# Expert stages of a fused fp32 kernel: A22 in the slots of w_in, sums in the slots of moe1, last output tiles one by one, another matmul step for the scheduler

## The chip, the cores and the metric

The kernel runs on one core of a Trainium2 chip. The metric is the device time of one execution in microseconds; one execution was also profiled, and all rows below are from that one. TensorE is called PE here, VectorE DVE, ScalarE ACT, GpSimd POOL, and the queue that issues the transfers SP.

## What is computed

Attention with a tanh cap on the scores, then two experts, one after the other, all in fp32 (cut from the reference; sizes in the comments):

```python
# q, k, v: 4 batches x 12 heads x 448 x 64
scores = cap * np.tanh(scale * np.matmul(q, k.transpose(0, 1, 3, 2)) / cap)
attn = softmax(scores) @ v                   # heads side by side: x, 1792 x 768
# expert 1, d_ff 2048
h = x @ w_in
y = (h * np.cos(h)) @ w_out
# expert 2, d_ff 1024
a = y @ w1
b = y @ w2
out = ((a * b) @ w3) @ w_out2
```

## The kernel before

A tile has 128 partitions; a batch's 448 tokens lie along the free axis, and the 768 columns of the model are six blocks of 128 rows. Each fp32 matmul is made of three fp32r ones: every operand is held as a rounded high half and the low rest (names ending in h and l), and `mm3` (L377) multiplies high by high, high by low and low by high. So every operand costs a conversion: a cast for the high half (on ACT, DVE or POOL) and a subtraction for the low one (on DVE or POOL), made by `halves`, `copy` (L353), `tt` (L363) and `lo` (L371).

The stages run in this order: attention (`columns`), with `make_w34` (L880 and on), which folds w3 and w_out2 of expert 2 into w34, beside it; `moe1`, expert 1; `moe2`, expert 2.

`moe1` goes through 32 units (a pair of blocks of d_ff, one batch). A unit makes h on PE, copies it into hs, and gets g = h cos h in a chain of DVE and ACT work (`chain`, L954 to L981): w from hs, kk and w less kk (the range reduction), a sine on ACT, times h, then the two halves of g. `y_part` adds g times w_out to y, two units later, and after a batch's last unit each of its six y blocks is stored to DRAM (y_d).

`moe2` takes y from y_d. It treats two batches at once (p = 0: batches 0 and 1, p = 1: batches 2 and 3) with a seven-product scheme: `lefts` makes the left operands A11, A12, S1 to S4 and A22 out of y and its sums, `rights` the right ones out of w1 and w2 for a block fc of d_ff, and `ab_step(p, fc)` multiplies them: seven products of nine matmuls, whose sums leave PSUM as tmp (copies) and c (the products a times b of the two batches, c11 and c21). `o_unit(b, fc)` converts c into the halves ab, loads w34[fc] through stq, and adds w34[fc] times ab to the six output blocks m of batch b, three matmuls each; after fc = 7 a block is copied into ob and stored (outT). For one batch of the pair the units run between the products of the next step, for the other behind the pair's last step.

No stage issues an instruction by itself. Everything goes into a `Plan` with a due time, a cost for each engine that can do it, and its reads and writes. `schedule` plays the plan through with these costs and so fixes the order on each engine; PE's cost is counted in units of `MM`, its time for one matmul of 448 columns. A ring is a number of equal slots; an operation that needs a slot of a full ring waits, in the plan and on the chip. Rings lie in pools, and a pool opens only after every user of the pools that it takes the place of is done (`swap`): mp (weights, hs, w and g of moe1), yp (y) and wi (w_in) close together, and q2 opens in their place. q2 holds what only `moe2` has: stq, rawq, A22's halves, w34, ab, c, tmp and ob. The pool lp (rawl, stl and the other left operands) opens earlier. The lines that decide it are three:

```python
swap("wp", opens=("yp", "mp", "cv"))
swap("cv", "attn", opens=("lp",))
swap("mp", "yp", "wi", opens=("q2",))
```

Of the kernel before, what the change touches and what calls it, by code (L numbers as in the profile page):

```python
# [10 lines left out]
F32 = mybir.dt.float32  # L11
# [317 lines left out]
def program(  # L329
# [52 lines left out]
    MM = S / 2400 + 0.017  # L382
# [10 lines left out]
    for name, kw in dict(const={}, xring={}, dram=dict(space=DRAM), psum=dict(space=PSUM), attn={}, lp={},  # L393
                         wi=dict(side="right"), wp=dict(side="right"), yp=right, mp=right, cv=right,
                         q2=right).items():
        pool(name, **kw)
# [474 lines left out]
    def make_w34():  # L871
# [12 lines left out]
        for k, (fc, p) in enumerate(runs):  # L884
# [9 lines left out]
            for n in range(2):  # L894
                half = slice(n * (DM // 2), (n + 1) * (DM // 2))
                acc = hy_r.ref()
                for q, jc in enumerate(jcs):
# [5 lines left out]
                    plan.op(due + n * 4 + q, [("PE", 3 * (DM / 4800 + 0.017), f)], r=[*w3, *wo[jc]], w=[acc])  # L903
# [15 lines left out]

    def moe1(raw_r, x_r):  # L920
# [3 lines left out]
        hs_r, w_r = (ring("mp", t, [P, 2, S], F32, 2) for t in ("hs", "w"))  # L924
        kk_r = ring("mp", "kk", [P, S], F32, 1)
        g_r = ring("mp", "g", [P, 2, 2, S], F32R, 2, 16)
        y_r = ring("yp", "y", [P, KD, S], F32, 2)
# [105 lines left out]
        for u in (n - 2, n - 1):  # L1033
            for m in range(KD):
                y_part(u, m, unit_due(n) + ((u - n + 2) * KD + m) * pu / 12)
# [10 lines left out]
    KH, HALF = KD // 2, DM // 2  # L1046
# [4 lines left out]
    def moe2():  # L1051
        raws = [ring("lp", "rawl", [P, 2 * DM], U32, 1), ring("q2", "rawq", [P, 2 * DM], U32, 1)]
        sts = [ring("lp", "stl", [P, DM], F32, 4), ring("q2", "stq", [P, DM], F32, 2)]
        left_r = {x: hl("q2" if x == "A22" else "lp", f"y{x}", [P, KH, S], 1, 16 * (x == "A22")) for x in LEFT}
        w34_r, ab_r = hl("q2", "w34", [P, DM], 3), ring("q2", "ab", [P, 2, S], F32R, 3, 16)
        c_r, tmp_r, ob_r = (ring("q2", t, [P, S], F32, n) for t, n in (("c", 11), ("tmp", 6), ("ob", 5)))
        V0, AB, OU = unit_due(4 * NP) + G["pu"], 63 * MM, 18 * MM
        left, right, cs = {}, {}, {}

# [4 lines left out]
        def lefts(p, due, step, raw_r, st_r, late=False):  # L1064

            for x in LEFT:
                if (x == "A22") == late:
                    left[p, x] = [r.new() for r in left_r[x]]
            for k in range(KH):
                t = due + k * step  # L1070

                def to(x, src, at):
                    halves(at, [z.at(k, lambda t, k=k: t[:, k, :]) for z in left[p, x]], src, S)
# [5 lines left out]
                if late:  # L1079
                    a22 = st_r.ref()[:, :S]  # L1080
# [22 lines left out]
        def rights(p, fc, due):  # L1103

            x = [sts[0].ref(), sts[0].ref()]
            for a in range(2):
                z = w12_d.at((fc, a), lambda d, a=a: d[fc, a])
                if p == 0:
                    convert(due + 2 * a, raws[a if fc else 0], x[a], w12[fc, a], DM)
# [24 lines left out]
        def product(p, fc, i, bank, first, due):  # L1134
# [4 lines left out]
            def f():  # L1139
                xt = [z.tile() for z in x]  # L1140
                wt = [seg(z, j, 1) for z in w]
                for k in range(KH):
                    c = slice(k * P, (k + 1) * P)
                    mm3(bank()[:, :S], wt[0][:, c], wt[1][:, c], xt[0][:, k, :], xt[1][:, k, :],
                        first and k == 0, k == KH - 1, on=not first)

            plan.op(due, [("PE", 9 * MM, f)], r=[*(z.at(k) for z in x for k in range(KH)), *(z.at(2 * (j // 2)) for z in w)],
                    w=[bank])

        def ab_step(p, fc, due, between):  # L1150
# [3 lines left out]
            def out(bank, when):  # L1154
                x = tmp_r.ref()
                copy(when, x, bank[:, :S], S, "AD", psum=True)
                return x

            p1 = hy_r.ref()
            product(p, fc, 0, p1, True, at[0])  # L1160
            s1 = out(p1, at[1])
            p2 = hy_r.ref()
# [123 lines left out]
```

## Time and profile before

| | |
|---|---|
| median of 3 runs | 1114.83 us (1112.88 to 1116.92) |
| profiled execution, its own time | 1116.46 us |
| its span | 1114.7 us |
| mean granted TensorE clock | 0.993 |
| PE busy | 1078.9 us, 97%, 5040 matmuls |
| DVE busy | 885.6 us, 79% |
| ACT busy | 498.4 us, 45% |
| POOL busy | 156.1 us, 14% |

The span is the time from the first to the last event of the profiled execution, and its own time is 1.8 us more. Shares of busy time are means over stages with different limits. PE is the engine with almost no idle, so the places to look at are those where a row of PE shows idle time ahead of it, with the operation that ended it, and those where the granted clock is below 1.00 (0.50 is 1.2 of 2.4 GHz).

### The profile page before, as it was taken

The page shows a single profiled execution, that of the slowest core. Times are in us where ns is not written, and L with a number is a line of the kernel's source. Part 1 is how long each engine was busy: PE and PEld are TensorE (multiplying, and loading weights), DVE is VectorE, ACT ScalarE, POOL GpSimd, SP SyncE. Part 2 cuts the span into 40 slices and gives each one's busy share as a digit, 9 for nine tenths or more (in the row PEclk, how much of TensorE's full clock was granted, in tenths as well). Part 3 has the DMA queues.
Part 4 walks back from the last instruction along what each step waited for, and adds up shares of the span by engine and source line. Part 5 has one row for each costly group of instructions (what it writes and reads, how often), then busy time and mean ns, then how long its engine had stood idle before and what let it go on. Part 6 is the DMA issues. An engine that isn't in the chain of part 4 may idle for free. (4 is left out here: it accounts for less than half of the span.)

```text
span 1114.7 us, 13997 instructions
## 1 busy us (share of the span) xinstructions
PE 1078.9 (97%) x5040; PEld 937.4 (84%) x5040; DVE 885.6 (79%) x1353; ACT 498.4 (45%) x656; POOL 156.1 (14%) x145
## 2 busy tenths in 40 slices
PE   5999999999999999999999999999899999999997
PEld 3777777777888888889999999999789998999996
DVE  6988767798998989868789977777699879767642
ACT  4887767677665656641253211111244334221121
POOL 2322111112331111101002000000122200100000
PEclk9999999999999999999999999999999999999998
DMA  9885766877755655426633411204456435421132
GB/s 238 231 221 158 207 186 170 228 192 238 236 165 158 185 151 174 160 75 213 231 124 110 138 48 57 57 15 154 154 184 198 157 116 188 159 85 58 58 107 81
DMA packets 95554, 169.04 MB, mean 152 GB/s; under 512 B 37362, under 2 KB 68850, under 8 KB 95474
## 3 DMA queue, kind: packets, MB, share of 16 engines
q1 hardware_dynamic: 95474, 168.05, 50.1%
q8 instruction: 41, 0.67, 0.3%
q14 instruction: 39, 0.32, 0.1%
HBM read 129.30 MB, written 38.62 MB: 151 GB/s over the span
## 5 line engine op out<-in xcount | busy, mean ns | idle before, releaser
L617 PE MATMUL bank<-p,v 112*128 112x448 f32 x384 | 160.9, 542 | 0.3 <-POOL raw L826 0.3
L606 ACT ACTIVATE double<-double,ts 112x896 f32<-112x896 f32 x96 | 94.1, 981 | 76.2 <-PE double L597 76.0
L378 PE MATMUL bank<-xh,wih 128*128 128x448 f32 x270 | 107.8, 399 | 2.7 <-DVE xh L355 2.2
L617 PEld LDWEIGHTS bank<-p,v 112*128 112x128 f32 x384 | 72.7, 191 | 41.3 <-issue 38.7
L378 PE MATMUL bank<-g,woh 128*128 128x448 f32 x260 | 100.7, 387 | 0.0
L379 PE MATMUL bank<-xl,wih 128*128 128x448 f32 x270 | 98.1, 363 | 0.2 <-DVE xl L364 0.2
L380 PE MATMUL bank<-xh,wil 128*128 128x448 f32 x270 | 98.0, 363 | 0.0
L606 ACT ACTIVATE p<-double,pac 112x896 f32<-112x896 f32 x96 | 96.8, 1011 | 2.4 <-PE bank L617 0.4
L380 PE MATMUL bank<-g,wol 128*128 128x448 f32 x260 | 94.2, 362 | 0.0
L379 PE MATMUL bank<-g,woh 128*128 128x448 f32 x260 | 94.1, 362 | 0.0
L596 PE MATMUL double<-qh,ks 128*112 128x448 f32 x192 | 72.8, 379 | 13.6 <-DVE ks L364 9.5
L364 DVE TENSOR_TENSOR y<-bank,y 128x448 f32<-128x448 f32 x111 | 68.5, 617 | 21.8 <-PE bank L380 21.3
L597 PE MATMUL double<-ql,ks 128*112 128x448 f32 x192 | 71.7, 373 | 0.0
L378 PEld LDWEIGHTS bank<-xh,wih 128*128 128x128 f32 x270 | 50.7, 188 | 11.7 <-issue 5.0
L379 PEld LDWEIGHTS bank<-xl,wih 128*128 128x128 f32 x270 | 50.8, 188 | 8.8 <-issue 5.2
L378 PE MATMUL bank<-w2h,w3h 128*128 128x384 f32 x128 | 57.5, 449 | 0.0
L831 POOL TENSOR_SCALAR wx<-rawc 128x768 f32<-128x768 f32 x29 | 33.7, 1164 | 165.9 <-DVE wil L364 81.7
L354 ACT COPY hs<-bank 128x448 f32<-128x448 f32 x39 | 20.8, 533 | 77.0 <-PE bank L380 76.9
L379 PEld LDWEIGHTS bank<-g,woh 128*128 128x128 f32 x260 | 48.8, 188 | 6.7 <-issue 3.5
L378 PEld LDWEIGHTS bank<-g,woh 128*128 128x128 f32 x260 | 48.8, 188 | 6.6 <-issue 2.8
L380 PEld LDWEIGHTS bank<-xh,wil 128*128 128x128 f32 x270 | 50.8, 188 | 3.4
L976 ACT ACTIVATE w<-w 128x896 f32<-128x896 f32 x32 | 30.5, 953 | 50.5 <-DVE w L364 50.4
(286 smaller groups left out, 2831.7 us busy)
## 6 DMA issues: line engine op xcount, KB each, us to landing
rawc<-in_w_out SPq DMA_DIRECT2D x16, 768.0 KB, 5.9
stq<-w_d SPq DMA_DIRECT2D x32, 384.0 KB, 3.3
qr<-in_q SPq DMA_DIRECT2D x48, 224.0 KB, 5.2
kr<-in_k SPq DMA_DIRECT2D x48, 224.0 KB, 4.8
rawc<-in_w_in SPq DMA_DIRECT2D x13, 768.0 KB, 4.9
raw<-in_w3T SPq DMA_DIRECT2D x16, 512.0 KB, 5.9
rawl<-in_w SPq DMA_DIRECT2D x9, 768.0 KB, 4.5
raw<-in_w_out SPq DMA_DIRECT2D x8, 768.0 KB, 7.5
```

The source lines that it names most:

```text
L354: "A": ("ACT", (0.051 if psum else 0.094) + n / 1200, lambda: ACT.copy(dst(), src())),
L364: "D": ("DVE", 0.068 + n / 960, lambda: DVE.tensor_tensor(dst(), a(), b(), op=op))
L378: PE.matmul(out, wh, xh, start=first, stop=False, skip_group_check=on)
L379: PE.matmul(out, wh, xl, start=False, stop=False, skip_group_check=on)
L380: PE.matmul(out, wl, xh, start=False, stop=last, skip_group_check=on)
L596: PE.matmul(o, w, qh(), start=True, stop=False)
L597: PE.matmul(o, w, ql(), start=False, stop=True)
L606: lambda f=f, x=x, o=o: ACT.activation(o(), s(), f, scale=x[:CP]))],
L617: PE.matmul(pv()[:, :S], w()[:, 2 * c + n].rearrange("p a d -> p (a d)"), p()[:, n, :], start=c == 0 and n == 0, stop=c == NT - 1 and n == 1)
L831: lambda: POOL.tensor_scalar(x(), h_().bitcast(F32), 0.0, 1.0, op0=ALU.mult, op1=ALU.mult)),
L976: plan.op(due + 5, [("ACT", 0.094 + 2 * S / 1200, lambda: ACT.activation(w2(), w2(), AF.Sin, scale=TWOPI))], r=[w2], w=[w2], table="sin")
```

## The change

It joins the two expert stages in memory. The pools of w_in, y and a new one, hp, with hs and w, stay open to the end, and q2 takes the place of mp alone. A22's halves then lie in three slots of w_in's ring; the copies out of PSUM (tmp before) and the loads of A22 lie in halves of hs and w (`spares`); c lies in two y tiles at fixed places (`c_at`); ab is one tile of six parts, used in turn, and ob has three slots instead of five. The last unit's six `y_part` are handed to `moe2`, which plans them ahead of its own work. In `ab_step` the output blocks are planned between the products, not behind them. The last three units of the last batch (LAST = 3) are planned tile by tile: for each m the chunks fc = 5, 6 and 7, where all six m of one chunk came before the next. The raw w1 and w2 of fc = 1 both pass through rawl, where w2's passed through rawq. And two costs are set anew: `MM` from 0.2037 to 0.2000 us, and a matmul of w34 from 0.177 to 0.1733 us.

```diff
...
@@ -379,7 +380,7 @@
         PE.matmul(out, wh, xl, start=False, stop=False, skip_group_check=on)
         PE.matmul(out, wl, xh, start=False, stop=last, skip_group_check=on)
 
-    MM = S / 2400 + 0.017
+    MM = (S + 32) / 2400
     MT = CP / 1200 + 0.002
 
 
@@ -391,7 +392,7 @@
 
     right = dict(side="right", reuse_waits="tile")
     for name, kw in dict(const={}, xring={}, dram=dict(space=DRAM), psum=dict(space=PSUM), attn={}, lp={},
-                         wi=dict(side="right"), wp=dict(side="right"), yp=right, mp=right, cv=right,
+                         wi=dict(side="right"), wp=dict(side="right"), yp=right, hp=right, mp=right, cv=right,
                          q2=right).items():
         pool(name, **kw)
 
@@ -900,7 +901,7 @@
                         mm3(acc()[:, :DM // 2], w3[0]()[:, j], w3[1]()[:, j], wo[jc][0]()[:, half],
                             wo[jc][1]()[:, half], q == 0, q == NJ - 1)
 
-                    plan.op(due + n * 4 + q, [("PE", 3 * (DM / 4800 + 0.017), f)], r=[*w3, *wo[jc]], w=[acc])
+                    plan.op(due + n * 4 + q, [("PE", 3 * (DM / 4800 + 0.0133), f)], r=[*w3, *wo[jc]], w=[acc])
                 o = Ref(sums[fc], n, lambda t, half=half: t[:, half])
                 a = acc[:, :DM // 2]
                 if p == 0:
@@ -917,14 +918,15 @@
     def unit_due(u):
         return G["m0"] + min(u, G["ua"]) * G["pa"] + max(u - G["ua"], 0) * G["pu"]
 
+    y_r = ring("yp", "y", [P, KD, S], F32, 2)
+    hs_r, w_r = (ring("hp", t, [P, 2, S], F32, 2) for t in ("hs", "w"))
+
     def moe1(raw_r, x_r):
         cv = ring("cv", "rawc", [P, 2 * DM], U32, 2)
         wx = ring("mp", "wx", [P, DM], F32, 2)
         wo_r = hl("mp", "wo", [P, DM], 4)
-        hs_r, w_r = (ring("mp", t, [P, 2, S], F32, 2) for t in ("hs", "w"))
         kk_r = ring("mp", "kk", [P, S], F32, 1)
         g_r = ring("mp", "g", [P, 2, 2, S], F32R, 2, 16)
-        y_r = ring("yp", "y", [P, KD, S], F32, 2)
         w_t, g_t, yacc = {}, {}, {}
 
         groups = [(n, (b, b + 1)) for b in range(0, B, BH) for n in range(NP)]
@@ -1030,9 +1032,9 @@
                 chain(u, c, hp[:, :S], u0 + (c + 1) * pu / 2)
         n = len(units)
         weights(NG, unit_due(n) - G["wlead"])
-        for u in (n - 2, n - 1):
-            for m in range(KD):
-                y_part(u, m, unit_due(n) + ((u - n + 2) * KD + m) * pu / 12)
+        for m in range(KD):
+            y_part(n - 2, m, unit_due(n) + m * pu / 12)
+        return [lambda due, m=m: y_part(n - 1, m, due) for m in range(KD)]
 
     def mm_h(hp, wi, ks, xh_, xl_):
         def f():
@@ -1043,19 +1045,33 @@
         return f
 
 
-    KH, HALF = KD // 2, DM // 2
+    KH, HALF, LAST = KD // 2, DM // 2, 3
     LEFT = ("A11", "A12", "S2", "S1", "S3", "S4", "A22")
     RIGHT = ("B11", "B21", "T1", "T3", "T2", "T4", "B22")
     PRODUCTS = (("A11", "B11"), ("A12", "B21"), ("S2", "T2"), ("S1", "T1"), ("S3", "T3"), ("S4", "B22"), ("A22", "T4"))
 
-    def moe2():
+    def moe2(tail):
         raws = [ring("lp", "rawl", [P, 2 * DM], U32, 1), ring("q2", "rawq", [P, 2 * DM], U32, 1)]
         sts = [ring("lp", "stl", [P, DM], F32, 4), ring("q2", "stq", [P, DM], F32, 2)]
-        left_r = {x: hl("q2" if x == "A22" else "lp", f"y{x}", [P, KH, S], 1, 16 * (x == "A22")) for x in LEFT}
-        w34_r, ab_r = hl("q2", "w34", [P, DM], 3), ring("q2", "ab", [P, 2, S], F32R, 3, 16)
-        c_r, tmp_r, ob_r = (ring("q2", t, [P, S], F32, n) for t, n in (("c", 11), ("tmp", 6), ("ob", 5)))
+        left_r = {x: hl("lp", f"y{x}", [P, KH, S], 1) for x in LEFT if x != "A22"}
+        w34_r, abt = hl("q2", "w34", [P, DM], 3), ring("q2", "ab", [P, 6, S], F32R, 1, 16).new()
+        ob_r = ring("q2", "ob", [P, S], F32, 3)
+        abs_ = itertools.cycle(range(3))
         V0, AB, OU = unit_due(4 * NP) + G["pu"], 63 * MM, 18 * MM
         left, right, cs = {}, {}, {}
+
+        def spares():
+            for r in itertools.cycle((hs_r, w_r)):
+                it = r.new()
+                for n in range(2):
+                    yield it.at(n, lambda t, n=n: t[:, n, :])
+
+        spares = spares()
+        low, high = y_r.new(), y_r.new()
+
+        def c_at(b, fc):
+            it, n = (low, fc % 4) if b % 2 == 0 else (high, fc) if fc < KD else (low, fc - KD + 4)
+            return it.at(n, lambda t: t[:, n, :])
 
         def halves(due, z, src, n):
             copy(due, z[0], src, n, "ADP")
@@ -1065,19 +1081,23 @@
 
             for x in LEFT:
                 if (x == "A22") == late:
-                    left[p, x] = [r.new() for r in left_r[x]]
+                    if late:
+                        left[p, x] = [[r.ref()[:, :S] for _ in range(KH)] for r in wi_r]
+                    else:
+                        left[p, x] = [[z.at(k, lambda t, k=k: t[:, k, :]) for k in range(KH)]
+                                      for z in [r.new() for r in left_r[x]]]
             for k in range(KH):
                 t = due + k * step
 
                 def to(x, src, at):
-                    halves(at, [z.at(k, lambda t, k=k: t[:, k, :]) for z in left[p, x]], src, S)
+                    halves(at, [z[k] for z in left[p, x]], src, S)
 
                 def load(x, n, m):
                     src = y_d.at((2 * p + n, m), lambda d: d[2 * p + n, m])
                     dma(t - 4, x, src, r=[src], w=[x], kb=230)
 
                 if late:
-                    a22 = st_r.ref()[:, :S]
+                    a22 = next(spares)
                     load(a22, 1, k + KH)
                     to("A22", a22, t)
                     continue
@@ -1106,7 +1126,7 @@
             for a in range(2):
                 z = w12_d.at((fc, a), lambda d, a=a: d[fc, a])
                 if p == 0:
-                    convert(due + 2 * a, raws[a if fc else 0], x[a], w12[fc, a], DM)
+                    convert(due + 2 * a, raws[a if fc > 1 else 0], x[a], w12[fc, a], DM)
                     dma(due - 4, z, x[a], r=[x[a]], w=[z], kb=393, write=True)
                 else:
                     dma(due - 12, x[a], z, r=[z], w=[x[a]], kb=393)
...
         def ab_step(p, fc, due, between):
@@ -1152,40 +1172,48 @@
             at = [due + i * (AB + OU) / 7 for i in range(8)]
 
             def out(bank, when):
-                x = tmp_r.ref()
+                x = next(spares)
                 copy(when, x, bank[:, :S], S, "AD", psum=True)
                 return x
+
+            def then(i):
+                if i < len(between):
+                    between[i](at[i + 1] + 0.1)
 
             p1 = hy_r.ref()
             product(p, fc, 0, p1, True, at[0])
             s1 = out(p1, at[1])
+            then(0)
             p2 = hy_r.ref()
             product(p, fc, 1, p2, True, at[1])
-            c11 = c_r.ref()
+            c11 = c_at(2 * p, fc)
             tt(at[2], c11, p2[:, :S], s1, S, ALU.add, psum=True)
+            then(1)
             product(p, fc, 2, p1, False, at[2])
             u2 = out(p1, at[3])
+            then(2)
             p3 = hy_r.ref()
             product(p, fc, 3, p3, True, at[3])
             s5 = out(p3, at[4])
+            then(3)
             product(p, fc, 4, p1, False, at[4])
             tt(at[5], s5, p1[:, :S], s5, S, ALU.add, psum=True)
+            then(4)
             product(p, fc, 5, p3, False, at[5])
             tt(at[6], u2, p3[:, :S], u2, S, ALU.add, psum=True)
             tt(at[6] + 1, c11, c11, u2, S, ALU.mult, "DP")
+            then(5)
             product(p, fc, 6, p1, False, at[6])
-            c21 = c_r.ref()
+            c21 = c_at(2 * p + 1, fc)
             tt(at[7], c21, p1[:, :S], s5, S, ALU.mult, psum=True)
             cs[2 * p, fc], cs[2 * p + 1, fc] = c11, c21
-            for i, f in enumerate(between):
-                f(at[i + 1] + 0.1)
 
         acc = {}
 
         def o_unit(b, fc, due):
 
-            w, ab = pair(w34_r), ab_r.new()
-            ab = [ab.at(n, lambda t, n=n: t[:, n]) for n in range(2)]
+            w, n = pair(w34_r), 2 * next(abs_)
+            ab = [abt.at(k, lambda t, k=k: t[:, k, :]) for k in (n, n + 1)]
             f32(due, sts[1], w34_d.at(fc, lambda d: d[fc]), DM, *w)
             halves(due - 1.5, ab, cs[b, fc], S)
 
@@ -1213,6 +1241,8 @@
         out_i = Item(None)
         out_i.tile = lambda: None
         due = V0
+        for m, f in enumerate(tail):
+            f(due + (m - KD) * G["pu"] / 12)
         lefts(0, unit_due(21), 14.0, raws[0], sts[0])
         lefts(0, V0 + 2, 1.5, None, sts[1], late=True)
         for p in range(2):
@@ -1223,23 +1253,26 @@
             if p == 0:
                 lefts(1, due, 7.0, raws[1], sts[0])
                 lefts(1, due + 15, 3.0, None, sts[0], late=True)
-            for b, fc in [(2 * p, NF2 - 1)] + [(2 * p + 1, fc) for fc in range(NF2)]:
+            for b, fc in [(2 * p, NF2 - 1)] + [(2 * p + 1, fc) for fc in range(NF2 - LAST * p)]:
                 for m, f in enumerate(o_unit(b, fc, due)):
                     f(due + m * OU / KD)
                 due += OU
+        last = [o_unit(B - 1, fc, due + k) for k, fc in enumerate(range(NF2 - LAST, NF2))]
+        for m in range(KD):
+            for k, units in enumerate(last):
+                units[m](due + (LAST * m + k) * OU / KD)
 
 
     (queries if general else columns)()
     first = make_w34()
-    moe1(*first)
-    moe2()
-    swap("wp", opens=("yp", "mp", "cv"))
+    moe2(moe1(*first))
+    swap("wp", opens=("yp", "hp", "mp", "cv"))
     swap("cv", "attn", opens=("lp",))
-    swap("mp", "yp", "wi", opens=("q2",))
+    swap("mp", opens=("q2",))
     for _, f in plan.schedule():
         if f is not None:
             f()
-    for n in ("q2", "lp", "psum", "dram", "xring", "const"):
+    for n in ("q2", "hp", "yp", "wi", "lp", "psum", "dram", "xring", "const"):
         pools[n].close()
```

How the order moves. In the names below a number tells one slot from another; y_1716 and y_1718 are the y of one batch, y_1902 and y_1904 of another, hs_1518 and w_1530 the older of two slots of hs and w. First DVE, near the end of moe1's last unit; before:

```order
L364 TENSOR_TENSOR w_1650<-w_1650,kk_1530 128x448
L364 TENSOR_TENSOR y_1902<-double_76,y_1902 128x448
L355 CAST xh_1083<-stl_4015 128x768
L966 TENSOR_SCALAR w_1650<-hs_1646 128x448
L364 TENSOR_TENSOR xl_1091<-stl_4015,xh_1083 128x768
L364 TENSOR_TENSOR y_1902<-double_76,y_1902 128x448
L971 TENSOR_SCALAR kk_1530<-w_1650 128x448
L364 TENSOR_TENSOR y_1716<-bank_78,y_1716 128x448
L364 TENSOR_TENSOR w_1650<-w_1650,kk_1530 128x448
L364 TENSOR_TENSOR y_1716<-bank_80,y_1716 128x448
L364 TENSOR_TENSOR y_1716<-double_75,y_1716 128x448
L364 TENSOR_TENSOR w_1650<-w_1650,hs_1646 128x896
```

After, from the same subtraction on (wih and wil are the slots of w_in that become A22's halves):

```order
L365 TENSOR_TENSOR w_1651<-w_1651,kk_1533 128x448
L365 TENSOR_TENSOR wil_1363<-hs_1518,wih_1348 128x448
L365 TENSOR_TENSOR y_1904<-double_76,y_1904 128x448
L365 TENSOR_TENSOR wil_1264<-hs_1518,wih_1257 128x448
L356 CAST xh_1086<-stl_4016 128x768
L356 CAST wih_1309<-w_1530 128x448
L968 TENSOR_SCALAR w_1651<-hs_1644 128x448
L365 TENSOR_TENSOR wil_1326<-w_1530,wih_1309 128x448
L365 TENSOR_TENSOR y_1904<-double_76,y_1904 128x448
L973 TENSOR_SCALAR kk_1533<-w_1651 128x448
L365 TENSOR_TENSOR y_1718<-bank_80,y_1718 128x448
L365 TENSOR_TENSOR w_1651<-w_1651,kk_1533 128x448
```

Three subtractions and one cast of A22 now stand between this unit's range reduction and the last g; the cast out of w_1530 stands ahead of w<-hs.

SP, at the end of moe1, before (y_d<-y are the last stores of y, stq<-y_d the loads of A22, and rawl and rawq raw w1 and w2):

```order
L374 DMA w_d<-stl_4015 128x768
L374 DMA rawl_3843<-in_w 128x1536
L374 DMA y_d<-y_1716 128x448 x6
L374 DMA y_d<-y_1902 128x448 x6
L374 DMA rawq_5545<-in_w 128x1536
L374 DMA stq_5558<-y_d 128x448
L374 DMA stq_5562<-y_d 128x448
L374 DMA stq_5558<-y_d 128x448
```

After, at the same place:

```order
L375 DMA hs_1518<-y_d 128x448 x2
L375 DMA w_1530<-y_d 128x448
L375 DMA rawl_3839<-in_w 128x1536
L375 DMA w_d<-stl_4016 128x768
L375 DMA y_d<-y_1718 128x448 x6
L375 DMA w_d<-stl_4172 128x768
L375 DMA y_d<-y_1904 128x448 x2
L375 DMA rawl_3839<-in_w 128x1536
L375 DMA y_d<-y_1904 128x448 x3
```

The three loads of A22 go from behind the twelve stores to ahead of them, and two transfers for the weights come between the stores.

PE, the last twelve matmuls of the program, before (ab_5752 with w34h_5781 and w34l_5794 is the chunk fc = 7; double and bank are output blocks):

```order
L378 MATMUL double_76<-ab_5752,w34h_5781 128x448
L379 MATMUL double_76<-ab_5752,w34h_5781 128x448
L380 MATMUL double_76<-ab_5752,w34l_5794 128x448
L378 MATMUL bank_78<-ab_5752,w34h_5781 128x448
L379 MATMUL bank_78<-ab_5752,w34h_5781 128x448
L380 MATMUL bank_78<-ab_5752,w34l_5794 128x448
L378 MATMUL double_75<-ab_5752,w34h_5781 128x448
L379 MATMUL double_75<-ab_5752,w34h_5781 128x448
L380 MATMUL double_75<-ab_5752,w34l_5794 128x448
L378 MATMUL bank_80<-ab_5752,w34h_5781 128x448
L379 MATMUL bank_80<-ab_5752,w34h_5781 128x448
L380 MATMUL bank_80<-ab_5752,w34l_5794 128x448
```

After (w34h_5850, w34h_5637 and w34h_5733 belong to three chunks):

```order
L379 MATMUL double_76<-ab_5639,w34h_5850 128x448
L380 MATMUL double_76<-ab_5639,w34h_5850 128x448
L381 MATMUL double_76<-ab_5639,w34l_5853 128x448
L379 MATMUL bank_79<-ab_5639,w34h_5733 128x448
L380 MATMUL bank_79<-ab_5639,w34h_5733 128x448
L381 MATMUL bank_79<-ab_5639,w34l_5746 128x448
L379 MATMUL double_76<-ab_5639,w34h_5637 128x448
L380 MATMUL double_76<-ab_5639,w34h_5637 128x448
L381 MATMUL double_76<-ab_5639,w34l_5652 128x448
L379 MATMUL double_76<-ab_5639,w34h_5733 128x448
L380 MATMUL double_76<-ab_5639,w34h_5733 128x448
L381 MATMUL double_76<-ab_5639,w34l_5746 128x448
```

Before, four output blocks got their last chunk in these rows; after, two do, and the one on double_76 gets three chunks in a row. Ahead of `moe2`, PE's order is the same in both; in its first steps some products change places. POOL, over the whole program, has 17 subtractions and additions of two inputs where it had 10.

## Rows read from the trace of the kernel before

**Rows 1.** The page, busy time of PE over the span: us, share, instructions.

```profile
PE 1078.9 (97%) x5040; PEld 937.4 (84%) x5040; DVE 885.6 (79%) x1353; ACT 498.4 (45%) x656; POOL 156.1 (14%) x145
```

**Rows 2.** Windows: us, busy us per engine (instructions), granted clock, DMA share, GB/s.

```profile
775.00:800.00 25.00, 21.64 (x101) 19.16 (x100) 13.33 (x25) 6.04 (x10) 1.71 (x2) 0.95 0.47 155
800.00:825.00 25.00, 22.09 (x107) 19.47 (x106) 23.25 (x32) 10.09 (x17) 7.60 (x4) 0.98 0.58 193
825.00:900.00 75.00, 75.00 (x376) 70.10 (x375) 67.58 (x98) 28.21 (x42) 14.91 (x12) 1.00 0.52 172
...
797.70:801.10 3.40, 2.91 (x8) 1.77 (x6) 3.40 (x6) 1.67 (x2) 0.74 (x1) 0.50 0.46 128
```

**Rows 3.** PE's waits from 700 us on: us in total, times, longest.

```profile
PE double L380 <- DVE w34l L364: 1.5, 1, 1.5
...
PE double L379 <- DVE g L364: 0.5, 1, 0.5
PE double L379 <- DVE ab L364: 0.5, 1, 0.5
```

**Rows 4.** Timeline of PE: start, us, line, operation [idle before, what ended it].

```profile
223.91 0.49 PE L378 MATMUL bank<-xh,wih 128*128 128x448 f32 x1 [2.23 <-DVE xh L355]
...
776.69 0.36 PE L378 MATMUL bank<-yA11h,xh 128*128 128x448 f32 x1
776.89 0.36 PE L379 MATMUL bank<-yA11l,xh 128*128 128x448 f32 x1
...
795.28 0.47 PE L378 MATMUL bank<-yA22h,xh 128*128 128x448 f32 x1 [2.83 <-DVE yA22h L355]
796.28 0.48 PE L379 MATMUL bank<-yA22l,xh 128*128 128x448 f32 x1 [0.53 <-DVE yA22l L364]
...
821.19 0.36 PE L378 MATMUL double<-yS1h,xh 128*128 128x448 f32 x1
...
936.55 0.47 PE L380 MATMUL bank<-ab,w34l 128*128 128x448 f32 x1 [1.73 <-DVE w34l L364]
...
1105.95 0.37 PE L380 MATMUL bank<-ab,w34l 128*128 128x448 f32 x1
```

**Rows 5.** Timeline of SP, start and us, and landing of the loads into stq.

```profile
763.63 14.23 SPq L374 DMA_DIRECT2D y_d<-y  x12
...
778.43 12.56 SPq L374 DMA_DIRECT2D stq<-y_d  x3
...
DMA to landing us min/median/max: 3.0/4.4/4.5
```

**Rows 6.** Timeline of DVE, moe1's last unit and the start of moe2.

```profile
756.28 1.07 DVE L364 TENSOR_TENSOR g<-w,g 128x896 fp32r<-128x896 f32 x1
...
760.98 0.39 DVE L966 TENSOR_SCALAR w<-hs 128x448 f32<-128x448 f32 x1 [0.38 <-ACT hs L354]
...
765.30 0.62 DVE L364 TENSOR_TENSOR y<-double,y 128x448 f32<-128x448 f32 x1 [0.58 <-PE double L380]
...
768.44 1.08 DVE L364 TENSOR_TENSOR g<-w,g 128x896 fp32r<-128x896 f32 x1
...
784.16 0.62 DVE L364 TENSOR_TENSOR c<-double,tmp 128x448 f32<-128x448 f32 x1 [6.65 <-PE double L380]
```

**Rows 7.** The end: last copy on ACT, the stores on SP, their landing.

```profile
1107.09 0.53 ACT L354 COPY ob<-bank 128x448 f32<-128x448 f32 x1 [0.65 <-PEq L324]
...
1103.95 4.03 SPq L374 DMA_DIRECT2D outT<-ob  x6
...
DMA to landing us min/median/max: 2.1/3.6/4.3
```

**Rows 8.** Timeline of POOL and DVE; group of w34l in moe2: busy us, mean ns.

```profile
817.32 2.09 POOL L366 TENSOR_TENSOR xl<-stl,xh 128x768 fp32r<-128x768 f32 x1 [1.76 <-ACT xh L354]
...
817.63 2.59 DVE L364 TENSOR_TENSOR w34l<-stq,w34h 128x768 fp32r<-128x768 f32 x1
...
L364 DVE TENSOR_TENSOR w34l<-stq,w34h 128x768 fp32r<-128x768 f32 x32 | 32.2, 1005 | 0.6
```

More of the change, by code (lines that the diff above doesn't have):

```diff
@@ L1 @@
 import heapq
+import itertools
 import math
@@ L1139, in f @@
             def f():
-                xt = [z.tile() for z in x]
+                xt = [[r() for r in z] for z in x]
                 wt = [seg(z, j, 1) for z in w]
@@ L1143, in f @@
                     c = slice(k * P, (k + 1) * P)
-                    mm3(bank()[:, :S], wt[0][:, c], wt[1][:, c], xt[0][:, k, :], xt[1][:, k, :],
+                    mm3(bank()[:, :S], wt[0][:, c], wt[1][:, c], xt[0][k], xt[1][k],
                         first and k == 0, k == KH - 1, on=not first)
-            plan.op(due, [("PE", 9 * MM, f)], r=[*(z.at(k) for z in x for k in range(KH)), *(z.at(2 * (j // 2)) for z in w)],
+            plan.op(due, [("PE", 9 * MM, f)], r=[*x[0], *x[1], *(z.at(2 * (j // 2)) for z in w)],
                     w=[bank])
```

## The prediction

> **What bounds the kernel now.** I read the busy shares first: PE is busy for 97% of the span [rows 1], so only places where PE waits, or runs at a low clock, and the ends of the span can give time. The next view was the table of windows around the start of expert 2, which begins at 776.69 us with the first product (out of yA11) [rows 4]. From 825 us on PE is busy for the whole 75 us; from 775 to 800 it is busy for 21.64 of 25 us and from 800 to 825 for 22.09, and in these two the mean granted clock is 0.95 and 0.98 [rows 2]. Then the list of what PE waited for from 700 us on, w34l, g and ab among it [rows 3], and the matmuls themselves with the idle ahead of them: the longest waits are those for A22 (2.83 and 0.53 us), at 795.28 and 796.28, and for w34l, at 936.55 [rows 4]. Nearly all of them stand in expert 2.
>
> The step from one matmul to the next is 0.20 us at full clock (776.69 to 776.89) [rows 4]. Expert 2 has 1584 matmuls, from 776.69 to the last one's start at 1105.95 [rows 4], which is 329.3 us where 316.6 would do: 12.7 us over. The largest part is the junction. In the order of before, 177 matmuls lie between the first product and the S1 product that starts at 821.19; they need 35.4 us and took 44.5 [rows 4]: **9.1 us over.** The idle on A22, 3.4 us, and on w34l, 1.5 us [rows 3], is the core of it; the rest is smaller waits, the restart after each wait, and a stretch from 797.7 to 801.1 us at the low clock (granted 0.50, which is 1.2 of 2.4 GHz, [rows 2]), in which a matmul steps 0.37 us instead of 0.20: 3.4 x (1 - 0.20/0.37) = 1.6 us. That stretch came 2.4 us after PE's idle of 2.83 us at 795.28 [rows 4].
>
> What ends that wait is a load. SP's twelve stores of y take from 763.63 to 777.9 us, and the three loads of A22 start only behind them, at 778.43, and are spread over 12.56 us [rows 5]; one takes 4.4 us to land, and there are two stq slots for three loads. Meanwhile DVE idles 6.65 us [rows 6], and then has the whole backlog to do: from 797.7 to 801.1 it is busy for all of 3.40 us [rows 2]. So the junction lacks no DVE time, it has it at the wrong place.
>
> **The change part by part.**
>
> A22 and the pools. The three loads now go into halves of hs and w, and the conversions into three wi slots, which exist before moe1 ends. In the new order SP issues them ahead of all twelve y stores, and DVE converts them in moe1's last unit. PE needs A22 only 12.6 us after the first product, so the waits of 2.83 and 0.53 us go, and the low clock behind them with them. What is late next? I put DVE's new rows behind the first product with the durations of the trace (0.62 us for 448 columns, [rows 6], and 1.0 for 768, [rows 8], each a tenth less where one follows the other directly): the backlog is done some 5 us after the first product, c11 at 12.1, w34l at 15.1 and ab's low half at 15.7, while PE comes to it at 16.4. That is a slack of 0.7 us, so I keep 0.4 us of stall for a slip. Of 9.1 us over, 0.4 stays.
>
> The bill for it stands in moe1's last unit. Three low halves and one high half come onto DVE there, at most 3 x 0.62 + 0.39 = 2.2 us, between the g of one unit (756.28) and the g of the next (768.44) [rows 6]. DVE idles 0.38 and 0.58 us in that stretch [rows 6], so 1.3 us is left at most, and PE already waits 0.5 us for that g [rows 3]: every us there counts. Besides, the cast out of w waits for w's own DMA, which can be issued only after the g at 756.28 has read w (1.07 us): about 757.5, plus a landing of 3.0 to 4.5 us, as for stq [rows 5], so 760.5 to 762.0; and w<-hs, which starts the last chain of g at 760.98, stands behind that cast. The cost is 0.6 to 1.8 us; I take 1.0. Junction: 9.1 - 0.4 - 1.0 = **7.7 us gained.**
>
> The sums in halves of hs and w, c in two y tiles, ab in one tile. Same instructions at the same durations; what changes is when a slot is free. From 825 to 900 us, with eleven c and six tmp, PE is full and DVE busy for 67.58 of 75 us [rows 2], a slack of 1.6 us per 16.2 us step (seven products and six output matmul groups). The order of after keeps the pattern of products and evictions there. I cost it at nothing, and price a failure below.
>
> The joint between batches 0 and 1 (900 to 945 us). PE waits there 0.5 us for ab [rows 3] and 1.73 us for w34l, at 936.55 [rows 4]. A wait costs some 0.27 us more than its idle: the two A22 waits at 795.28 and 796.28 are 1.00 us apart where 0.20 would do, for an idle of 0.53. So the two are 2.7 us now. Between the last product of the pair and the first of the next, DVE's rows add up to 38.2 us before, and to 35.2 in the new order, because some casts of ab and w34 move to ACT, against 36.0 us of PE's work: about 0.7 us of stall is left, **2.0 us gained.** The fewer ob slots (three for five) pull the other way: the fourth copy must wait until the first has landed, 4 us or so; the bank it frees is needed 0.6 us after that by the order, so I leave it at nothing here, with 2 us in the range. What is left of expert 2's excess, 12.7 - 9.1 - 2.7 = 0.9 us of small waits, I take as half gone: 0.4.
>
> The tail. Now all six output tiles finish within the last 3.6 us; the six stores are issued from 1103.95 over 4.03 us [rows 7], the sixth copy runs at 1107.09 after an idle of 0.65 us, since it needs a slot of ob again, and the stores land in 2.1 to 4.3 us [rows 7]. From the last matmul's start to the span's end (1114.7) it is 8.75 us, and some 3.1 us of this lie behind the last landing (about 1107.6 + 4.0 = 1111.6). In the new order the tiles finish 1.2 to 1.8 us apart, one at a time, so the last store meets an empty queue: 0.37 for the matmul, 0.2 + 0.53 for the copy, 0.3 to issue, 2.1 to 3.6 to land, 3.1 fixed, which is 6.6 to 8.1. I take 6.85: **1.9 us gained.** PE pays nothing for it: the three chunks have their w34 and ab before they are needed, with 1.4 us to spare for the last.
>
> The scheduler's step. Before expert 2, PE's order is word for word the same. DVE, ACT and POOL trade some instructions from about 45 us on. The wait that matters there, 2.23 us for xh at 223.91 [rows 4], has the same rows around it in the new order, so it stays. The part before 700 us has hardly any other wait, so it can lose as well as win: 0, with 2 us either way.
>
> **Sum**, against the profiled execution (1116.46 us, span 1114.7): -7.7 - 2.0 - 0.4 - 1.9 = -12.0, so 1104.5. The median of the runs is 1114.83 and they go from 1112.88 to 1116.92, so the profiled one is a little on the high side; I take 0.5 off: **1104 us.**
>
> **Rivals.**
>
> *A new wait takes the place of the old.* The last unit of moe1 is where DVE is tight. If w lands at the late end and y's evictions queue up behind the cast, PE's wait for g goes from 0.5 to 3 us or so, with the size of the wait that brought the low clock at 797.7 (2.83), and so 1.6 us more: 1104 + 1.5 + 1.6 + a late ab (1.5) = 1108.5. For it: in-order DVE, a wait for a DMA ahead of the g chain. Against it: the load is small and SP is idle ahead of it.
>
> *GpSimd holds DVE.* At 817.32 a two-input subtraction on POOL runs for 2.09 us, and beside it DVE's w34l, also with two inputs, takes 2.59 us, where the 32 of expert 2 take 1.0 us on average [rows 8]; PE then waits 1.5 us for it [rows 3]. The new order gives POOL 17 such two-input instructions instead of 10. If three of the seven new ones meet DVE at a tight place, at 1.5 us and 0.27 each, that is 5.3 us: 1109.5. The Trainium skill ("SBUF — State Buffer", section "Who interferes with whom") says that a VectorE instruction with two SBUF inputs contends with a GpSimd instruction that reads SBUF, and that the later one is fully blocked for the whole instruction; the row agrees, since DVE ended 0.8 us after POOL did. By that rule every such meeting would cost what this one did; by the trace most of them cost nothing, since from 825 to 900 us POOL is busy for 14.91 us and PE waits for nothing.
>
> *Slower than before: the sums' slots hold up every step.* The halves of hs and w come free in pairs, when both are read, and c and ab sit at fixed places. If a copy out of PSUM has to wait for such a slot once per step, DVE's slack of 1.6 us is used up first and the rest falls on PE. It takes 14 us of PE time to come out slower than before by 0.3%, about 1.0 us in each of the 15 steps after the first, so 2.6 us of blocking a step; at 1.2 us of PE time it is 1104 + 18 = 1122. Against it: the order of evictions is the one that filled PE before, and a sum lives for less than one step, with eight halves for the three that are alive.
>
> *The change doesn't do what it says.* If the A22 loads are held by something other than the order shows, such as the release of hs, the junction stays and only tail and joint gain: 1116.5 - 4.3 = 1112.
>
> **How the numbers follow.** Two runs of this kernel differ by up to 0.3%, 3.3 us, so faster means below about 1111.5 and slower above 1118. Chances: the forecast with its bounds (1100 to 1107) 0.62; the new wait 0.15, GpSimd 0.12, both still faster; the change without effect at the junction, or both rivals at once, 0.06; slower 0.05. The range takes the forecast, the first two rivals and, below, a tail and an early part that do better: 1099 to 1111. Faster 0.87, same 0.08, slower 0.05.
>
> **What would show it.** Right: the A22 loads ahead of the y stores and no PE wait for A22; granted clock 1.00 from 775 to 825 us; S1 of the third step some 36 us after the first product; a wait of 1 to 2 us for g near 769 us; one output store at a time at the end, and 6.6 to 7.2 us from the last matmul to the span's end. Wrong: PE waits for w34l or ab that recur every 16 us, a wait for g above 2.5 us with a clock of 0.5 behind it, or new waits before 700 us.

## The result, and the profile after

The changed kernel takes 1130.94 us (median of 6 runs, 1128.33 to 1133.15) against 1114.78 us before (6 runs, 1112.88 to 1117.11): a ratio of 1.0144, with a 95% interval of 1.0124 to 1.0163. It is slower by 16 us, where 1104 us were forecast. Its profiled execution took 1128.33 us, with a span of 1126.5 us.

The windows of the changed kernel that answer to [rows 2] (columns as there):

```profile
775.00:800.00 25.00, 24.44 (x121) 22.19 (x119) 20.29 (x28) 10.57 (x16) 6.91 (x5) 1.00 0.60 211
800.00:825.00 25.00, 21.68 (x100) 18.28 (x101) 19.63 (x29) 6.92 (x11) 5.70 (x6) 1.00 0.46 158
825.00:900.00 75.00, 67.17 (x307) 55.52 (x305) 57.14 (x80) 18.83 (x29) 13.47 (x12) 1.00 0.43 145
900.00:925.00 25.00, 23.15 (x105) 19.09 (x105) 13.81 (x26) 4.80 (x9) 0.42 (x1) 1.00 0.21 63
```

The first line is the gain that was forecast: at the start of expert 2 PE does 121 matmuls in 25 us instead of 101, at the full clock. The next lines are a loss that was not: from 825 to 900 us PE does 307 matmuls where it did 376, and DVE is busy for 57.14 us instead of 67.58. Neither is busier; both wait, at a granted clock of 1.00. The loss ends before the second pair of batches: from 950 to 1075 us PE is busy for 124.07 of 125 us.

What PE waits for from 775 us on (us in total, times, longest):

```profile
PE double L379 <- DVE y L365: 7.3, 9, 2.0
PE double L379 <- DVE hs L365: 3.2, 3, 1.7
PE double L379 <- DVE w L365: 1.2, 4, 0.6
PE double L379 <- ACT w L355: 0.7, 1, 0.7
PE double L379 <- ACT hs L355: 0.7, 1, 0.7
PE double L379 <- DVE hs L356: 0.2, 1, 0.2
```

No w34l, no ab, no A22 [rows 3, 4]: every wait is that of a product which goes into a double PSUM tile, for an operation that reads a sum out of PSUM (line 379 is the first matmul of a product's three). They come back in every step. The idle adds up to 13.3 us, and a wait costs more than its idle: behind the one that ends at 851.19 (below) the next matmul starts 0.31 us later instead of 0.20. From the timeline of PE, the starts of expert 2, of the steps fc = 2 and fc = 7 of p = 0, and of the last matmul:

```profile
774.96 0.37 PE L379 MATMUL bank<-yA11h,xh 128*128 128x448 f32 x1
...
807.29 0.47 PE L379 MATMUL double<-yA11h,xh 128*128 128x448 f32 x1 [2.05 <-DVE y L365]
...
905.70 0.47 PE L379 MATMUL double<-yA11h,xh 128*128 128x448 f32 x1
...
1117.81 0.36 PE L381 MATMUL double<-ab,w34l 128*128 128x448 f32 x1
```

The five steps from fc = 2 to fc = 6 take 98.4 us, 19.7 us each, where a step has 81 matmuls or 16.2 us. Now one piece of such a step, from the timelines of PE, ACT and DVE; the last matmul of A11, the last of A12, the copy of A11's sum (tmp before, now a half of w), c11 (now in a y tile), and the next product:

```profile
847.75 0.36 PE L381 MATMUL double<-yA11h,xl 128*128 128x448 f32 x1
...
849.55 0.36 PE L381 MATMUL double<-yA12h,xl 128*128 128x448 f32 x1
...
849.94 0.54 ACT L355 COPY w<-double 128x448 f32<-128x448 f32 x1 [2.87 <-PE double L381]
...
850.51 0.62 DVE L365 TENSOR_TENSOR y<-double,w 128x448 f32<-128x448 f32 x1 [0.65 <-ACT w L355]
...
851.19 0.47 PE L379 MATMUL double<-yS2h,xh 128*128 128x448 f32 x1 [0.69 <-DVE y L365]
```

A11 is done at 848.11 us. Its copy, on an ACT that has been idle for 2.87 us, starts at 849.94, 0.03 us after A12 is done, though it reads nothing of A12. S2 adds to A11's sum, and needs the copy alone; it starts when c11 has been read, which lies where A12 was. In the kernel before, the same copy starts 0.04 us after A11's last matmul, with A12 running:

```profile
848.59 0.36 PE L380 MATMUL bank<-yA11h,xl 128*128 128x448 f32 x1
...
848.99 0.53 ACT L354 COPY tmp<-bank 128x448 f32<-128x448 f32 x1 [2.18 <-PE bank L380]
```

The difference is in the PSUM tile. Before, one of the two products in flight lay in a bank that is a tile of its own, the other in a half of a double tile. In the changed kernel both lie in double_76, A11 in the one half and A12 in the other, in all steps of p = 0 from fc = 2 on. In the compiled program (this is the step fc = 4) the copy waits for the count of PE's semaphore that A12's last matmul brings, 3588, and S2 for that of c11: the two halves, two banks, are waited for as one. In the first kernel of the experiments below, with the same order of instructions and other tiles, the same copy waits for 3579, the count that A11's last matmul brings, and S2 for the copy. The order of the changed kernel has it to read, on PE (row numbers left out; the first matmul of each product):

```
L379 MATMUL double_76<-yA11h_3908,xh_1086 128x448
L379 MATMUL double_76<-yA12h_3963,xh_1086 128x448
L379 MATMUL double_76<-yS2h_4077,xh_1086 128x448
```

where before it was double_76, bank_80, double_76. So a product can't begin until the sum of the product before it has been read out, and no sum is read out beside a product any more.

So the wait stands in the program; the chip need not hold anything back for it. The Trainium skill ("PSUM — Partial Sum Buffer", section "PSUM bank collisions raise a hardware error") lets no two engines into the same bank at the same time, and says that accesses to different banks run clean. By that the wait between two banks of one tile is one of the program, not of the chip; the compiled program agrees.

### The profile page after: what moved, and what is told of

Its sections match the earlier page's. It is cut to its first block, busy times and chain, and to the rows that moved or that the text cites. A ratio compares the mean times of both kernels' runs of the same rounds, so it can differ in the third digit from the quotient of the medians.

```text
span 1126.5 us, 14022 instructions
## 1 busy us (share of the span) xinstructions
PE 1085.0 (96%) x5040; PEld 933.7 (83%) x5040; DVE 879.0 (78%) x1338; ACT 503.6 (45%) x663; POOL 157.9 (14%) x153
## 4 chain that ended last, share of the span: by engine, by line
PE 81%; DVE 11%; DMA 4%; issue 1%; ACT 1%; SPq 1%; POOL 0%; DVEq 0%; ACTq 0%; POOLq 0%
PE bank L380 12%; PE bank L379 12%; PE bank L381 12%; PE double L379 11%; PE double L380 10%; PE double L381 10%; PE bank L618 9%; PE double L597 3%; PE double L598 2%; DMA kr<-in_k 2%; DVE y L365 2%; DVE w L365 1%; DMA rb<-rs_d 1%; SPq L375 1%; DVE xl L365 1%
## 5 line engine op out<-in xcount | busy, mean ns | idle before, releaser
L355 ACT COPY hs<-double 128x448 f32<-128x448 f32 x40 | 21.4, 534 | 130.9 <-PE double L381 122.9
L832 POOL TENSOR_SCALAR wx<-rawc 128x768 f32<-128x768 f32 x29 | 30.9, 1066 | 164.0 <-DVE wil L365 72.0
```

The costliest lines, as they stand in the source:

```text
L355: "A": ("ACT", (0.051 if psum else 0.094) + n / 1200, lambda: ACT.copy(dst(), src())),
L832: lambda: POOL.tensor_scalar(x(), h_().bitcast(F32), 0.0, 1.0, op0=ALU.mult, op1=ALU.mult)),
```

## The experiments

**Theory T**: two products in the halves of one PSUM tile are waited for as one. **Rivals**: S, the slots of the sums in halves of hs and w, of c and of ab hold DVE up (the prediction's slower case); G, POOL's two-input instructions hold DVE up.

**Banks apart, and the opposite in the kernel before.** The first kernel is the changed one with another choice among the PSUM slots that are free at the time; the order of instructions on every engine stays.

```diff
-                    it.slot = heapq.heappop(it.ring.free)[1]
+                    free_now = [x for x in it.ring.free if x[0] <= t + 1e-9]
+                    got = min(free_now, key=lambda x: (it.likes.index(x[1]) if it.likes else 0, x))
+                    it.ring.free.remove(got)
+                    heapq.heapify(it.ring.free)
+                    it.slot = got[1]
...
             p1 = hy_r.ref()
+            p1.item.likes = (4, 5, 6, 7, 0, 1, 2, 3)
...
                         acc[m] = hy_r.ref()
+                        acc[m].item.likes = (0, 1, 2, 3, 4, 5, 6, 7)
```

(p2 and p3 as p1; 0 to 3 are the halves of the double tiles.)

> The changed kernel, with one thing altered: which free PSUM slot an operation of expert 2 gets. Products prefer the four banks that are tiles of their own, output blocks prefer the four halves of the two double tiles. The order of instructions on every engine is the one of the changed kernel. Theory T (two halves of one PSUM tile are waited for as one, so from the third step of p = 0 on each product waits until the product before it has been read out): the 19.7 us of a step of p = 0 fall back to 16.2, six steps, 21 us, with 2 to 3 more ahead of them: 1107 us, 1104 to 1110. Rival S (the slots in halves of hs and w, of c and of ab hold up DVE): no change, 1128 to 1133. Rival G (POOL's two-input instructions hold DVE): no change, 1128 to 1133.

Measured: 1105.7 us (4 runs), ratio to before 0.9904 (0.9884 to 0.9924). The steps of p = 0 take 16.2 to 16.35 us, PE is full in the window again, and no wait of PE is left from 780 us to the end:

```profile
825.00:900.00 75.00, 75.00 (x376) 70.20 (x375) 65.58 (x97) 21.32 (x33) 14.24 (x11) 1.00 0.46 153
```

The second kernel is the one before, with the preferences the other way round (products 2, 3, 0, 1, 4 to 7; blocks 4 to 7, 0 to 3).

> The kernel before, order of instructions unchanged, with the opposite preference: products prefer the halves of the double tiles, output blocks the single banks. In the whole of p = 1 the two products in flight then lie in the two halves of one double tile (47 successions), in p = 0 in halves of two different ones. Theory T: p = 1 gets slower, p = 0 stays; with 3.4 us a step as in the changed kernel's p = 0 that would be 7 x 3.4 = 24 us, with DVE less loaded in p = 1 (74% against 90%) somewhat less: 1130 to 1139 us. Rivals S and G: same as before, within 0.3%.

Measured: 1138.59 us, ratio 1.0205 (1.0185 to 1.0224). The loss now stands where the pair lies in one tile: the steps of p = 1 from fc = 2 on take 19.0 to 21.7 us where they took 16.2, and those of p = 0 still take 16.2 to 16.5. Expert 2 takes 354.6 us instead of 329.3, and 21.6 of these 25.4 us are those of p = 1. Most of the rest, 3.1 us, is lost in the first two steps of p = 0, where seven successions lie in one tile too. PE's longest waits in that kernel from 950 us on:

```profile
PE double L383 <- DVE c L369: 5.1, 7, 0.8
PE double L383 <- DVE tmp L369: 3.2, 7, 1.8
```

T stands by both: the same slots for sums, c and ab, the same POOL instructions and the same order are fast or slow by the tile alone. S and G fall.

**Which edit it was.** In the changed kernel without the new place of the output units in `ab_step`, no two successive products share a tile; in the kernel before with that edit alone, 43 do.

```diff
             cs[2 * p, fc], cs[2 * p + 1, fc] = c11, c21
+            for i in range(6):
+                then(i)
```

(and the six calls of `then` between the products taken out.)

> The changed kernel with one edit undone: in ab_step the output units are again planned behind the seven products instead of between them. The slot of an output block is taken in the order in which the plan lists the operations, so the blocks get other slots: no two successive products lie in halves of one tile. The order on PE is the changed kernel's. Theory T and this edit as its cause: 1104 to 1109 us, as e1_banks_apart. If the edit is not the cause, or if the position of the units costs by itself: 1128 to 1133.

Measured: 1102.84 us (4 runs, 1102.35 to 1105.42), ratio 0.9894 (0.9875 to 0.9913). The same two places in its timelines:

```profile
838.68 0.36 PE L381 MATMUL bank<-yA11h,xl 128*128 128x448 f32 x1
...
839.08 0.53 ACT L355 COPY w<-bank 128x448 f32<-128x448 f32 x1 [2.22 <-PE bank L381]
...
841.28 0.36 PE L379 MATMUL bank<-yS2h,xh 128*128 128x448 f32 x1
```

The copy runs beside A12, and S2 starts on PE's step. The order on PE is not quite the changed kernel's: A12 and S2 change places in the second step of each pair of batches, and DVE, ACT and POOL trade some work. So this run shows what the edit does, and banks apart what the tiles do alone.

> The kernel before with this edit alone: the output units planned between the products. 43 successions of products in p = 0 then lie in the two halves of one tile (45 in the changed kernel, none in the kernel before). Theory T: six steps of p = 0 at 19.7 us instead of 16.2, 21 us and a few more: 1133 to 1140 us. If the change's slots for sums, c and ab were needed for the loss (rivals S and G): within 0.5% of the kernel before.

Measured: 1143.82 us (1140.01 to 1146.85), ratio 1.0258 (1.0226 to 1.0291), some 4 us above the upper end of what was expected. Its steps of p = 0 take 19.6 to 22 us from fc = 2 on, and the start of expert 2 loses besides: PE does 72 matmuls from 775 to 800 us (101 before), at a mean clock of 0.86. So the edit alone costs 29 us in the old kernel, and the change's other parts gave 13 of them back. The link is the plan: a ring hands out its slots in the order in which the operations are listed, so listing an output block between two products moves later products to other banks. In most steps the order on PE shows it in nothing but the tile's name.

**The early loads of A22.**

```diff
-                    a22 = next(spares)
+                    a22 = st_r.ref()[:, :S]
```

> As e1_banks_apart, but A22 of batches 0 and 1 is loaded through the two stq slots, as in the kernel before, so the loads can start only when mp is done and q2 opens; the conversions still go to slots of w_in, and all else is as in e1_banks_apart. If the early loads of A22 are what repaired the start of expert 2 (it takes 318.3 us in e1_banks_apart, 329.3 in the kernel before), a part of the 9 us comes back: PE waits for A22 again, 3 to 9 us slower than e1_banks_apart, 1109 to 1115. If the repair came from the rest (c, sums and ab elsewhere, another order of products): within 1 us of e1_banks_apart.

Measured: 1114.42 us, 8.7 us above banks apart, and no different from before (ratio 1.0007, 0.9993 to 1.0021). SP issues the loads at 774.47 and 784.90, and PE waits for A22 again:

```profile
792.51 0.47 PE L384 MATMUL bank<-wih,xh 128*128 128x448 f32 x1 [4.08 <-DVE wih L361]
...
775.00:800.00 25.00, 18.67 (x80) 15.36 (x78) 18.56 (x27) 8.04 (x12) 5.38 (x6) 0.87 0.61 217
```

Expert 2 takes 330.3 us, against 318.3 with the banks apart and 329.3 before. So nearly the whole gain of the change hangs on where these three loads go: the slots in hs and w exist in time, those in q2 don't.

**The tail.**

```diff
-    KH, HALF, LAST = KD // 2, DM // 2, 3
+    KH, HALF, LAST = KD // 2, DM // 2, 0
```

(on top of banks apart.)

> As e1_banks_apart, with LAST = 0: the last three chunks again chunk by chunk, as in the kernel before. The prediction's tail term says 1.9 us slower than e1_banks_apart. What the profile of the changed kernel shows speaks against it: there 8.7 us lie between the last matmul's start and the span's end, as in the kernel before (8.75), with the data of the last store through some 5 us ahead of the end. By that, the end is a fixed chain behind the last issue on SP, and the term is only the 0.65 us that the last copy waited: 0.3 to 0.9 us slower than e1_banks_apart.

Measured: 1106.28 us, 0.6 us above banks apart, inside both kernels' scatter. In the profiled execution it is 10.9 us instead of 8.65 from the last matmul's start to the span's end: with three slots of ob a copy at the end waits 1.46 us for a store. Expert 2 takes 0.7 us less, so from the first product on it is 1.5 us longer than banks apart. The first product comes 1.1 us earlier, which is no work of the edit: in the three kernels with the same order up to there (changed, banks apart, this one) it starts at 774.96, 777.33 and 776.19 us. The median can't tell the term from nothing.

> As e1_banks_apart, without the last part of the program: the test of cap, the branch and the second version of the program for large caps, which is not executed with these inputs, are left out. It measures what lies behind the last store. Theory B (a fixed chain of the program's end, the load of the flag, the branch and the jump, takes the time, not the store's landing): 8.65 us from the last matmul's start to the span's end shrink by 2 to 4 us, 1102 to 1104 us in all. The prediction's reading (copy, issue, landing, then 3.1 us that belong to every program): 8.65 stays, within 0.5 us.

Measured: 1099.92 us, 5.8 us below banks apart, more than expected. From the last matmul's start (1093.72) to the span's end (1097.6) it is 3.9 us, 4.8 less than 8.65. Only this part is sure to be the end's: the two kernels were timed beside other runs of the kernel before (medians 1115.06 and 1114.27), and the first product comes 1.95 us earlier in this profile. The last store is issued by 1095.06 and lands 1.9 us later, 0.6 us ahead of the end:

```profile
1086.84 8.22 SPq L371 DMA_DIRECT2D outT<-ob  x6
```

With the fallback, the end comes 5.8 to 7.4 us after the last issue in the nine kernels that have it, whether the last stores landed in 1.9 to 3 us (banks apart) or in 2.1 to 4.3 [rows 7]. The landing is covered by the program's end. What in that end takes the time isn't shown: with the fallback each engine loads the flag and branches, and a load takes 0.5 us (the flag itself is made near 494 us, in three rows of DVE that are left out too).

**The scheduler's step alone**, in the kernel before:

```diff
-    MM = S / 2400 + 0.017
+    MM = (S + 32) / 2400
...
-                    plan.op(due + n * 4 + q, [("PE", 3 * (DM / 4800 + 0.017), f)], r=[*w3, *wo[jc]], w=[acc])
+                    plan.op(due + n * 4 + q, [("PE", 3 * (DM / 4800 + 0.0133), f)], r=[*w3, *wo[jc]], w=[acc])
```

> The kernel before with the scheduler's two new costs alone (0.2000 for a matmul, 0.1733 for one of w34). Its products of expert 2 never lie in two halves of one tile. If the costs are what moved the 1.7 us ahead of expert 2 (the changed kernel reaches its first product at 774.96 us instead of 776.69, without the low clock behind 224 us), they bring 1 to 3 us here: 1112 to 1114. If they did harm: above 1118.

Measured: 1113.14 us (10 runs), ratio 0.998 (0.997 to 0.999): a gain of 1.9 us. In the profiled execution expert 2 takes 327.6 us, 1.7 less than before, and no wait for xh near 224 us is left.

## Why the prediction was wrong

**The step that failed** is the second part of the change: "Same instructions at the same durations; what changes is when a slot is free", and "The order of after keeps the pattern of products and evictions there. I cost it at nothing". The order does keep the pattern; it does not keep the tiles. Of a PSUM tile I read that it was there, not which one: the names double_76 and double_76 where before it was bank_80 and double_76. Six steps at 3.5 us more and some 3 us ahead of them make about 24 of the 24.5 us by which expert 2 takes longer than with the banks apart (342.9 against 318.3); the medians lie 25 us apart.

**The rival that ended on the right side** gave 1122 us for 1.2 us of PE time per step, at a chance of 1 in 20. That is luck: it put the loss in all 15 steps after the first, where it stands in those of p = 0 alone, its size per step was a third of the 3.5 us measured, and no slot of hs, w, c or ab was waited for. Against it I held that PE was full with the same pattern before, which is the same oversight once more. The arguments that DVE had slack were true, and of no use: DVE idled more than before (57.14 of 75 us busy), since each eviction and each product waited for the other.

**The other steps**, read from the kernel with the units behind, where nothing covers them:

- Junction and joint. Expert 2 takes 317.4 us from its first product (775.75) to the last matmul's start (1093.18), against 329.3 before [rows 4]: 11.8 us gained, where the terms made 8.7 + 2.0 + 0.4 = 11.1. No low clock (1.00 from 775 to 825 us), no wait for w34l or ab. Right, and the run with A22 through stq shows that the cause was right too. A part of the 11.8 may be the scheduler's step, which alone brought expert 2 to 327.6.
- The wait for g was 0.7 us in the changed kernel, from 0.5 [rows 3], where 1.0 us more was allowed. SP issued w's load at 754.94, right behind the g that reads w, as reckoned (this g comes 2.4 us earlier than before), and it had landed when DVE came to its cast at 759.14. A wait of 0.5 us for y came besides.
- The tail, forecast as a gain of 1.9 us, is the term that was mis-sized: 8.69 us after, 8.75 before, 7.7 with the units behind. I took 3.1 us as fixed behind the last landing. What there is are 5.8 to 7.4 us behind the last issue, and the landing lies beside it.
- The scheduler's step, taken at 0 with 2 us either way, gave 1.9 us in the kernel before; in the changed kernel it wasn't undone alone. The wait for xh, which was to stay at 2.23 us, was 1.4 there.
- GpSimd: its two-input instructions stretch some DVE rows of expert 2 (with the banks apart, a low half of ab at 792.45 takes 1.45 us, where the 32 take 0.65 on average), and in the two kernels with the tiles apart PE waits for none of them.

The sum of the terms, 1104, is about what the changed kernel would have been with its products in other tiles: 1105.7 and 1102.84 us. That it comes so close is in part luck: the tail gave 1.0 us or less where 1.9 were forecast, and the scheduler's step, taken at 0, gave about as much as the tail lacked.

## What to carry to other kernels

When an order is compared, compare the tiles as well as the operations: where the program's waits are kept by tile, two results in flight in the parts of one PSUM tile make every reader wait for the other part's writer, and the trace then shows short waits in every round, with neither engine busier. Give things that are read and written at the same time tiles of their own, and prefer the double tiles for what is only read at the end. A product that shares its double tile with an output block lost nothing here: with the units behind, one copy starts at 846.28, behind the block's three matmuls (done at 846.24) and not behind the product (845.64), and PE waits for none. Where slots are handed out in the order of a list, moving a line in the list is a change of placement.

## What the runs showed that was not expected

The end of the program, with a branch to a version that isn't taken, costs some 5 us here (4.8 of them between the last matmul and the span's end), and hides what the last stores cost. And a placement of banks alone, without one instruction moved, is worth 25 us of 1131 in one kernel (1130.94 to 1105.7) and 24 us of 1115 in the other (1115.06 to 1138.59).
